# An attention and gated-MLP kernel: own places in SBUF for the first chunk's q, k and v, its k issued from ScalarE's queue, and a retuned order of work

## The chip, the cores and the metric

The kernel runs on one core of a Trainium2 chip. The metric is the device time of one execution in microseconds; three runs of the kernel before gave 740.18, 741.96 and 742.35 us, median 741.96 us. A profiled execution gives a trace of every instruction on the core's engines: PE (TensorE, matrix products and transposes; PEld are its weight loads), DVE (VectorE), ACT (ScalarE), POOL (GpSimd) and SP (SyncE, which here only issues transfers).

## What is computed

Attention over 4 batches, 8 heads, 768 positions and a head size of 64, masked to a causal window of 128 positions plus 4 sink positions; then its output, as 3072 tokens of 512 numbers, goes through a dense layer of 512 x 2048, the gate h * cos(h), and a second dense layer of 2048 x 512. Cut to what matters:

```python
scores = scale * np.matmul(q, k.transpose(0, 1, 3, 2))
keep = is_sink | in_window
scores = np.where(keep, scores, -1000000000.0)
a = np.exp(scores - np.max(scores, axis=-1, keepdims=True))
a = a / (np.sum(a, axis=-1, keepdims=True) + 1e-09)
x = np.matmul(a, v).transpose(0, 2, 1, 3).reshape(B * S, H * D)
h = x @ w_in
g = h * np.cos(h)
return g @ w_out
```

q, k and v arrive as float32, the two weights as 64-bit floats, decoded to float32 on the chip.

## The kernel before

The tokens are worked in 12 chunks of 256. For each chunk the attention of 8 heads is done, in pairs of heads, and then the dense part, in 8 slots of 256 hidden columns each. A slot is 24 products of the first layer (`h_mm`, L419), the gate on ACT and DVE (L428 to L464), and 24 products of the second layer (`out_mm`, L479). Each float32 operand is split into a high and a low part, and three products stand for one. Chunk 0 is an exception: its second layer uses unsplit float32 (L474), because the second weights are split only later.

The first three chunks are the "early" ones: they are the first 256 tokens of batches 0, 1 and 2, 24 heads in all. For a pair of early heads, q and k are loaded in rows (`load_natural`, L817, two transfers each), turned by PE (`pe_turn`, L825), copied out of PSUM (`q_out`, `k_out`, both through the helper at L407 for ACT and L409 for DVE), multiplied to scores (`scores_pe`, L850), masked on DVE (L919), exponentiated on ACT (L928), normalised (`norm`, L947; ACT L951, DVE or POOL L953), turned again (L1025), copied (L407, L409) and multiplied with v (L1077). Other chunks work per head, with split operands (L906, L1021, L1101).

All pairs share one tile for q (`xq`), one for k (`xk`) and one for v (`v32`): a load for the next pair waits until PE has turned the present one. All of these loads are issued by SP.

At the same time the weights are loaded in 32 pieces of 512 KB (`weight_piece`, L524), decoded by three instructions on DVE (L540, L546, L552) and split by one on ACT (L579) and one on DVE or POOL (L582).

The order in which each engine does this is not written by hand. A planner (`Plan.order`, L70) takes steps with a list of engines that may do them, an estimated duration, what they depend on, and a due time; it runs through time and gives each engine, as it comes free, the step with the smallest due time of those that are ready. The due times and the penalties for a choice of engine are worked out from the table `C` (L28). 160 small products of no use (`fill`, L1375, tile `idle`) have the latest due times of all, so they stand wherever the planner sees PE with nothing else to do. On the chip each engine runs its list in order, and waits by semaphores.

The first product of the dense part (slot 0) writes the PSUM bank `b4`, which the turned probabilities of every odd head of chunk 0 use before; so it comes after the last head of chunk 0 is turned and copied out.

Of the kernel before, what the change touches and what calls it, by code (L numbers as in the profile page):

```python
# [9 lines left out]
F32 = mybir.dt.float32  # L10
# [17 lines left out]
C = {  # L28
# [3 lines left out]
    "NWF": 0.232, "PB": 5, "PEN": 27.684, "PL": 3, "POOLF": 4.428, "POOLPEN": -1.361, "QE": 5.937, "R": 2, "RAW": 2,  # L32
# [3 lines left out]
}  # L36
# [133 lines left out]
def attn_moe_kernel(ctx, tc, q, k, v, n_sink, window, w_in, w_out, out):  # L170
# [401 lines left out]

    def split_piece(plan, prio, w, ready, before):


        add = plan.add

        def round_hi(e):
            nc.scalar.copy(out=w.high(), in_=w.w32)  # L579

        def rest_lo(e):
            e.tensor_tensor(out=w.low(), in0=w.w32, in1=f32(w.hi), op=ALU.subtract)  # L582

        s4 = add((("ACT", act(WP)),), round_hi, [ready], prio)
        return [s4, add(sub(WP), rest_lo, [s4, *before], prio, port=True)]
# [87 lines left out]
    def banded_path():  # L673
# [119 lines left out]
        def load_v_pair(o, o1):  # L793
            def fn(e):
                dst = v32_t.rearrange("p a n d -> p (a n d)")[:, : o.nkb * 2 * D]
                o.v2 = o1.v2 = dst.rearrange("p (n c) -> p n c", c=2 * D)
                for h in range(2):
                    nc.sync.dma_start(
                        out=dst.rearrange("p (n h d) -> p n h d", n=o.nkb, d=D)[:, :, h, :],
                        in_=v[o.b, o.h + h, o.kb0 * P : (o.kb0 + o.nkb) * P, :].rearrange("(n s) d -> s n d", s=P),  # L800
                    )
            return fn
# [9 lines left out]
        def load_natural(tile, src, n):  # L812
# [5 lines left out]
            return fn  # L818

        def pe_turn(o, part, tile, n):  # L820
            def fn(e):
                if part == 0:
                    o.qk = ps.tile([P, 2, NT], F32, name=f"qk_{o.tag}", tag="b3")
                for m in range(n):
                    nc.tensor.transpose(  # L825
                        out=o.qk[:, part, m * P : (m + 1) * P],
                        in_=tile.rearrange("p a b -> p (a b)")[:, m * 2 * D : (m + 1) * 2 * D], identity=ident,
                    )
            return fn
# [310 lines left out]
        first = None  # L1140
        vs_last = None
        waiting = []

        def before_softmax(g, o):
# [19 lines left out]
            if o.early:  # L1164
                if o.odd == 0:
                    bx, bb, o.btq = buf("xq", 1), buf("b3", 1), buf("tq", 1)
                    src = lambda c: q[o.b, o.h + c, o.i0 * P : o.i0 * P + NT, :]
                    i = add(dma(2), load_natural(xq_t, src, CB), [bx], t - 8 * T + DQ + 0.4 if g else -2000.0, lat=2.3)
                    i = qt = add([("PE", 0.23)], pe_turn(o, 0, xq_t, CB), [i, bb], t - 6 * T + DQ + 0.3)
                    bx.users.append(i)  # L1170
                    q0 = add([("ACT", act(NT, False)), ("DVE", dve(NT))], q_out(o), [i, o.btq], t - 6 * T + DQ + 0.6)
                    bb.users.append(q0)
                    bx, o.bkz = buf("xk", 1), buf("kz", 1)
                    src = lambda c: k[o.b, o.h + c, o.kb0 * P : (o.kb0 + o.nkb) * P, :]
                    i = add(
                        dma(2), load_natural(xk_t, src, o.nkb), [bx], t - 7 * T + DQ + 1.2 if g else -1999.0, lat=2.4
                    )
                    i = add(
                        [("PE", 0.115 * o.nkb)], pe_turn(o, 1, xk_t, o.nkb), [i, qt],
                        t - 6 * T + DQ + 1.0,  # L1180
                    )
                    bx.users.append(i)
                    kk = []
# [90 lines left out]
        def after_softmax(g, o):  # L1274
            x, t = xs[o.a], head_time(g)
            T, DV, DA = (C["TQ"], C["VE"], C["AE"]) if o.early else (C["T"], C["DV"], C["DA"])
            if o.early and o.odd == 0:
                o.bxs = [buf("v32", C["XV"]) for _ in range(C["XV"])]
                o.vl = add(dma(2), load_v_pair(o, heads[g + 1]), o.bxs, t - 2 * T + DV + 3.2, lat=2.4)
# [4 lines left out]
            if o.early:  # L1284
# [12 lines left out]
                )  # L1297
                x.y0 = y0
                for bx in bxs:
                    bx.users.append(y0)  # L1300
# [116 lines left out]
        for t, a, s in slots:  # L1417
# [4 lines left out]
            for m in range(0 if a else FG):  # L1422
                f = s * FG + m
                prio = slot_time(1, s) + C["SO"] + C["SO2"] * m
                pair = split_piece(plan, prio, w_outs[f], w_out_ready[s][f], before["out"])
                before["out"] = pair + xs[0].om[f]
# [181 lines left out]
```

## Time and profile before

| what | us |
|---|---|
| median of three runs | 741.96 |
| the profiled execution | 743.21 |
| span of its trace | 741.5 |
| PE busy in the span | 724.8 |
| DVE busy | 627.9 |
| ACT busy | 557.7 |
| POOL busy | 106.6 |

The span goes from the first to the last instruction of the program. Busy is the time in which an engine works on at least one instruction; on PE the ends of products are modelled and neighbours overlap, so the distance from one start to the next tells more than the duration of one. The granted clock of TensorE is full in every slice until the last few microseconds.

### The profile page before, as it was taken

What the parts mean: (1) busy time and instruction counts of PE and PEld (TensorE: products, weight loads), DVE (VectorE), ACT (ScalarE), POOL (GpSimd) and SP (SyncE); (2) the same over time, 40 slices, a digit from 0 to 9 for tenths busy, and PEclk for the clock granted to TensorE, in tenths of its full rate; (3) what the DMA queues carried; (4) which work ended last, traced back from release to release, by engine and by line L of the source; (5) the groups of instructions that cost most, each with busy time, mean ns of one, the idle gap of its engine ahead of it and who ended that gap; (6) DMA issues with size and microseconds to landing.
All of it is one profiled execution on the core that took longest, in us unless ns stands there. A gap on an engine that the chain in (4) does not pass through costs nothing.

```text
span 741.5 us, 15107 instructions
## 1 busy us (share of the span) xinstructions
PE 724.8 (98%) x4827; PEld 645.5 (87%) x4827; DVE 627.9 (85%) x1778; ACT 557.7 (75%) x1387; POOL 106.6 (14%) x191
## 2 busy tenths in 40 slices
PE   9989999999999999999999999999999999999996
PEld 8777776799999998998998889999998999999995
DVE  6899999877899999999999999897988888965432
ACT  4889969556979778799797898887888698884322
POOL 1000000001121221212212122122001122212000
PEclk9999999999999999999999999999999999999999
DMA  5755566132355455465465442232342232110000
GB/s 148 199 169 185 165 179 171 55 49 41 97 144 130 97 149 135 99 171 120 113 157 159 95 106 52 56 67 42 53 88 48 45 80 51 33 40 8 30 1 32
DMA packets 215896, 71.48 MB, mean 96 GB/s; under 512 B 204288, under 2 KB 204800, under 8 KB 215808
## 3 DMA queue, kind: packets, MB, share of 16 engines
q1 hardware_dynamic: 215376, 70.36, 39.1%
q8 instruction: 40, 0.66, 0.4%
q14 instruction: 48, 0.39, 0.2%
q10 hardware_dynamic: 432, 0.07, 0.0%
HBM read 64.10 MB, written 6.29 MB: 95 GB/s over the span
## 4 chain that ended last, share of the span: by engine, by line
PE 80%; DVE 9%; ACT 7%; DMA 1%; issue 1%; POOL 0%; SPq 0%; DVEq 0%; POOLq 0%; ACTq 0%
PE h L419 33%; PE acc L479 31%; PE av L1101 5%; PE s L906 4%; PE tp L1021 2%; PE idle L1379 1%; ACT p L928 1%; ACT p L951 1%; DVE p L919 1%; DVE w_out L546 1%; PE acc L474 1%; DVE w_out L552 1%; PE av L1077 1%; DVE lo_in L582 1%; ACT r L441 1%
## 5 line engine op out<-in xcount | busy, mean ns | idle before, releaser
L419 PE MATMUL h<-xhi,hi_in 128*128 128x256 f32 x768 | 226.0, 294 | 2.6 <-ACT firsts L407 1.4
L419 PE MATMUL h<-xlo,hi_in 128*128 128x256 f32 x768 | 217.0, 282 | 0.4 <-DVE xlo L365 0.4
L419 PE MATMUL h<-xhi,lo_in 128*128 128x256 f32 x768 | 216.7, 282 | 0.0
L419 PEld LDWEIGHTS h<-xhi,hi_in 128*128 128x128 f32 x768 | 146.0, 190 | 7.8 <-DVE glo L464 1.8
L419 PEld LDWEIGHTS h<-xhi,lo_in 128*128 128x128 f32 x768 | 146.3, 191 | 3.2 <-issue 1.1
L419 PEld LDWEIGHTS h<-xlo,hi_in 128*128 128x128 f32 x768 | 146.1, 190 | 0.6 <-DVE xlo L365 0.6
L479 PE MATMUL acc<-hi_out,ghi 128*128 128x512 f32 x350 | 142.2, 406 | 0.2 <-ACT raw L407 0.2
L479 PE MATMUL acc<-lo_out,ghi 128*128 128x512 f32 x350 | 137.4, 393 | 0.0
L479 PE MATMUL acc<-hi_out,glo 128*128 128x512 f32 x350 | 137.4, 392 | 0.0
L1060 POOL TENSOR_SCALAR_AFFINE_SELECT pz<-pz 128x512 fp32r<-128x512 f32 x128 | 83.4, 652 | 285.1 <-DVE pz L1047 221.0
L919 DVE CUSTOM_DVE_ANT_0 p<-s,mk 128x264 f32<-128x264 f32 (+1 forms) x192 | 75.7, 401 | 24.9 <-PE s L906 19.8
L428 ACT ACTIVATE yt<-h 128x512 int32<-128x512 f32 x96 | 57.2, 596 | 49.9 <-PE h L419 49.4
L928 ACT ACTIVATE p<-p,st 128x264 f32<-128x264 f32 (+1 forms) x192 | 93.6, 491 | 0.6
L434 DVE SCALAR_TENSOR_TENSOR r<-h,yt 128x512 f32<-128x512 f32 x96 | 65.5, 683 | 25.8 <-ACT yt L428 25.5
L441 ACT ACTIVATE r<-r,neg 128x512 f32<-128x512 f32 x96 | 69.3, 724 | 13.9 <-DVE r L434 13.1
L479 PEld LDWEIGHTS acc<-hi_out,glo 128*128 128x128 f32 x350 | 65.8, 188 | 14.8
L479 PEld LDWEIGHTS acc<-hi_out,ghi 128*128 128x128 f32 x350 | 65.9, 188 | 8.7 <-ACT raw L407 0.7
L479 PEld LDWEIGHTS acc<-lo_out,ghi 128*128 128x128 f32 x350 | 66.1, 189 | 7.6
L464 DVE TENSOR_TENSOR glo<-h,ghi 128x512 fp32r<-128x512 f32 x88 | 60.1, 683 | 11.6 <-ACT ghi L458 10.9
L446 DVE TENSOR_TENSOR h<-h,r 128x512 f32<-128x512 f32 x88 | 60.4, 687 | 8.2 <-ACT r L441 8.0
L458 ACT CAST ghi<-h 128x512 fp32r<-128x512 f32 x88 | 51.3, 583 | 16.1 <-PE acc L479 12.9
L906 PE MATMUL s<-r,l 128*128 128x264 f32 (+2 forms) x288 | 59.6, 288 | 0.8 <-DVE st L919 0.7
(140 smaller groups left out, 1288.5 us busy)
## 6 DMA issues: line engine op xcount, KB each, us to landing
raw<-in_moe_w_in_dram SPq DMA_DIRECT2D x32, 512.0 KB
raw<-in_moe_w_out_dram SPq DMA_DIRECT2D x32, 512.0 KB
xk<-in_k_dram SPq DMA_DIRECT2D x256, 48.0 KB
v<-in_v_dram SPq DMA_DIRECT2D x64, 96.0 KB
out_dram<-raw SPq DMA_DIRECT2D x22, 256.0 KB
xq<-in_q_dram SPq DMA_DIRECT2D x144, 32.0 KB
v<-in_v_dram SPq DMA_DIRECT2D x32, 64.0 KB
xq<-in_q_dram SPq DMA_DIRECT2D x24, 64.0 KB
```

The source lines that it names most:

```text
L419: nc.tensor.matmul(out=o.h[:, t, :], lhsT=w[:, fs], rhs=xx[:, c, :], start=(c == 0 and n == 0), stop=(c == NC - 1 and n == 2),)
L428: nc.scalar.activation(out=yt, in_=o.h, func=AF.Copy, scale=INV2PI, bias=0.25)
L434: nc.vector.scalar_tensor_tensor(out=o.r, in0=o.h, scalar=INV2PI, in1=yt, op0=ALU.mult, op1=ALU.subtract)
L441: nc.scalar.activation(out=o.r, in_=o.r, func=AF.Sin, scale=TWOPI_DOWN, bias=quarter)
L446: nc.vector.tensor_tensor(out=o.h, in0=o.h, in1=o.r, op=ALU.mult)
L458: nc.scalar.copy(out=o.ghi, in_=o.h)
L464: e.tensor_tensor(out=o.glo, in0=o.h, in1=f32(o.ghi), op=ALU.subtract)
L479: nc.tensor.matmul(out=x.acc[j], lhsT=gg[:, t, j * P : (j + 1) * P], rhs=w, start=(f == 0 and n == 0), stop=(f == NFT - 1 and n == 2), ski ...
L906: nc.tensor.matmul(out=o.s_ps[j][:, :w], lhsT=o.l[:, j * P : (j + 1) * P], rhs=r.rearrange("p n s -> p (n s)")[:, c0 : c0 + w], start=(n = ...
L919: nc.vector.tensor_tensor_reduce(out=o.p[:, j, :w], in0=o.s_ps[j][:, :w], in1=masks[min(o.i0 + j, 2)][:, :w], op0=ALU.add, op1=ALU.min, sc ...
L928: nc.scalar.activation(out=o.p[:, j, :w], in_=o.p[:, j, :w], func=AF.Exp, bias=o.lead.st[:, 0, o.nth, j : j + 1], scale=-1.0, accum_out=o. ...
L1060: nc.gpsimd.affine_select(out=env.pz4[:, :, :, n], in_=f32(env.pz4)[:, :, :, 0], pattern=[[0, 2], [0, CB], [sign, P]], compare_op=ALU.is_g ...
```

## The change

The first chunk's q and k of a pair get a tile of their own, and its v another (`early`). These tiles lie where the high parts of the last eight second weights come later (tags `a_out_8` to `a_out_15`), so the split of those weights (`split_piece`) now also waits for the last reader of the place (`rooms`). The loads of chunk 0 no longer wait for an earlier pair. Its q is issued by SP at due times of the table (`XP`), its k by ACT's queue ahead of its first work, its v by SP. The later early chunks keep the shared tiles. At the same time most numbers of the table `C` that set due times and the choice of engine are other ones; a few lines of it are shown.

```diff
-    "NWF": 0.232, "PB": 5, "PEN": 27.684, "PL": 3, "POOLF": 4.428, "POOLPEN": -1.361, "QE": 5.937, "R": 2, "RAW": 2,
-    "S0": -10.291, "S1": 61.51, "SAME": -0.554, "SE": -1.813, "SEM": 0.31, "SO": 6.105, "SO2": 1.36, "SPE": 0.183,
...
+    "NWF": 0.799, "PB": 5, "PEN": 24.474, "PL": 3, "POOLF": 12.358, "POOLPEN": -0.716, "QE": 8.165, "R": 2, "RAW": 2,
+    "S0": -10.709, "S1": 63.509, "SAME": -0.646, "SE": -1.186, "SEM": 0.209, "SO": 5.845, "SO2": 1.36, "SPE": 0.171,
...
+    "WO": 19.92, "WS": 1.465, "WS2": -0.01, "WT": 2, "XE": 2.209, "XP": [-2229.806, -1906.19, -1330.4, -570.267],
...
-        s4 = add((("ACT", act(WP)),), round_hi, [ready], prio)
+        s4 = add((("ACT", act(WP)),), round_hi, [ready, *room], prio)
...
-                dst = v32_t.rearrange("p a n d -> p (a n d)")[:, : o.nkb * 2 * D]
+                dst = (v32_t.rearrange("p a n d -> p (a n d)") if o.a else early(o, 1))[:, : o.nkb * 2 * D]
...
+        def early(o, n):
+            if not hasattr(o, "room"):
+                o.room = {}
+            if n not in o.room:
+                m = NFT - 2 * NP + 2 * o.pair + n
+                o.room[n] = wp.tile([P, WP], F32, name=f"room_{m}", tag=f"a_out_{m}")
+            return o.room[n]
+
+        def load_first(o, part, src, n):
+            def fn(e):
+                dst = early(o, 0)[:, part * NT : part * NT + n * 2 * D]
+                dst = dst.rearrange("p (n h d) -> p n h d", n=n, d=D)
+                for h in range(2):
+                    e.dma_start(out=dst[:, :, h, :], in_=src(h).rearrange("(n s) d -> s n d", s=P))
+            return fn
...
-                    i = add(dma(2), load_natural(xq_t, src, CB), [bx], t - 8 * T + DQ + 0.4 if g else -2000.0, lat=2.3)
+                    if o.a:
+                        i = add(dma(2), load_natural(xq_t, src, CB), [bx], t - 8 * T + DQ + 0.4, lat=2.3)
+                    else:
+                        i = add(dma(2), load_first(o, 0, src, CB), [], C["XP"][o.pair], lat=2.3)
...
+                    if o.a:
+                        i = add(dma(2), load_natural(xk_t, src, o.nkb), [bx], t - 7 * T + DQ + 1.2, lat=2.4)
+                    else:
+                        i = add([("ACT", 0.8)], load_first(o, 1, src, o.nkb), [], -2990.0 + o.pair, lat=2.4)
...
-                pair = split_piece(plan, prio, w_outs[f], w_out_ready[s][f], before["out"])
+                pair = split_piece(plan, prio, w_outs[f], w_out_ready[s][f], before["out"], rooms[f])
```

What this does to the lists of two engines stands in three places below. The first is the head of SP's list, the issues of transfers. `xq`, `xk` and `v` are the shared tiles, `room` the new ones, `raw` a weight piece as it comes from memory, `xb` the sink rows of v. Before:

```order
L817 DMA xq<-in_q_dram 128x2x64 x2
L817 DMA xk<-in_k_dram 128x2x64 x2
L532 DMA raw_70<-in_moe_w_in_dram 128x1024
L532 DMA raw_71<-in_moe_w_in_dram 128x1024
L798 DMA v_74<-in_v_dram 128x2x64 x2
L747 DMA xb<-in_v_dram 32x1x64 x4
L817 DMA xq<-in_q_dram 128x2x64 x2
```

And now:

```order
L835 DMA room_127<-in_q_dram 128x2x64 x2
L835 DMA room_130<-in_q_dram 128x2x64 x2
L835 DMA room_135<-in_q_dram 128x2x64 x2
L533 DMA raw_70<-in_moe_w_in_dram 128x1024
L533 DMA raw_71<-in_moe_w_in_dram 128x1024
L835 DMA room_156<-in_q_dram 128x2x64 x2
L818 DMA xq<-in_q_dram 128x2x64 x2
L818 DMA xk<-in_k_dram 128x2x64 x2
```

Three pairs' q now stand ahead of the first weight piece, and the four pairs' k have left this list for ACT's, where they stand behind the load of the exp table and the one small activation that follows it (L255 before), and ahead of all other work.

The second place is the head of PE's list, from the products of no use (`idle`) to the second pair's scores. `qk_0_0` is the PSUM tile of the first pair's turned q and k, `qk_0_2` that of the second; `s_0_0_0` and `s_0_0_1` are the two halves of the first pair's scores. Before:

```order
L1379 MATMUL idle<-gt 128x256 x8
L825 MATMUL qk_0_0_144<-ident,xq 128x128 x2
L1379 MATMUL idle<-gt 128x256 x7
L825 MATMUL qk_0_0_144<-ident,xk 128x128 x2
L1379 MATMUL idle<-gt 128x256 x13
L850 MATMUL s_0_0_0_188<-firsts,tq_0_0_154 128x2x128
L850 MATMUL s_0_0_1_192<-firsts,tq_0_0_154 128x512
L1379 MATMUL idle<-gt 128x256 x13
L825 MATMUL qk_0_2_218<-ident,xq 128x128 x2
L1379 MATMUL idle<-gt 128x256 x7
L825 MATMUL qk_0_2_218<-ident,xk 128x128 x2
```

And now:

```order
L1420 MATMUL idle<-gt 128x256 x8
L844 MATMUL qk_0_0_153<-ident,room_127 128x128 x2
L1420 MATMUL idle<-gt 128x256 x14
L844 MATMUL qk_0_0_153<-ident,room_127 128x128 x2
L1420 MATMUL idle<-gt 128x256 x11
L877 MATMUL s_0_0_0_212<-firsts,tq_0_0_161 128x2x128
L844 MATMUL qk_0_2_214<-ident,room_130 128x128 x4
L877 MATMUL s_0_0_1_222<-firsts,tq_0_0_161 128x512
L1420 MATMUL idle<-gt 128x256 x13
L877 MATMUL s_0_2_0_258<-firsts,tq_0_2_236 128x2x128
```

The second pair is turned right behind the first half of the first pair's scores, where 20 products of no use and the other half stood between; between the first pair's q and its k there are now 14 of them and not 7.

The third place is PE's list just ahead of slot 0's first product (`h`). `av` are the products with v of chunk 0's pairs, the one at L354 subtracts a pair's high part. Before, these are rows 71 to 79 of the list:

```order
L825 MATMUL qk_0_6_655<-ident,xq 128x128 x2
L1379 MATMUL idle<-gt 128x256
L850 MATMUL s_0_4_0_662<-firsts,tq_0_4_638 128x2x128
L354 MATMUL av_0_4_603<-xhi_397,gt 128x512
L825 MATMUL qk_0_6_655<-ident,xk 128x128 x2
L1379 MATMUL idle<-gt 128x256 x9
L1077 MATMUL av_0_6_698<-firsts,v_74 128x256
L1077 MATMUL av_0_6_698<-firsts,v_74 128x128
L419 MATMUL h_710<-xhi_397,hi_in_263 128x256
```

Now they are rows 56 to 64:

```order
L1052 MATMUL tp_0_7_566<-ident,p_0_7_410 128x128 x3
L1104 MATMUL av_0_4_540<-firsts,room_227 128x256
L1104 MATMUL av_0_4_540<-firsts,room_227 128x128
L877 MATMUL s_0_2_1_581<-firsts,tq_0_2_537 128x512
L1104 MATMUL av_0_6_589<-firsts,room_217 128x256
L1104 MATMUL av_0_6_589<-firsts,room_217 128x128
L355 MATMUL av_0_4_540<-xhi_427,gt 128x512
L1420 MATMUL idle<-gt 128x256 x8
L420 MATMUL h_613<-xhi_427,hi_in_282 128x256
```

Slot 0's first product has moved from row 79 to row 64: 108 of the 160 products of no use now stand ahead of it, where all 160 did. Of chunk 1's second pair of early heads (`s_0_2`) only the scores are done there, not those of the third (`s_0_4`). The other 52 stand behind it, all of them ahead of slot 4.

## Rows read from the trace of the kernel before

**Rows 1.** The page: busy us, share of the span and instructions of each engine.

```profile
span 741.5 us, 15107 instructions
PE 724.8 (98%) x4827; PEld 645.5 (87%) x4827; DVE 627.9 (85%) x1778; ACT 557.7 (75%) x1387; POOL 106.6 (14%) x191
```

**Rows 2.** Windows: stretch in us, its length, busy us and instructions per engine.

```profile
core 0: us, PE busy (x) PEld busy (x) DVE busy (x) ACT busy (x) POOL busy (x), PEclk, DMA share, GB/s
0.00:50.00 50.00, 45.21 (x286) 38.94 (x287) 40.53 (x141) 34.66 (x108) 3.24 (x12) 1.00 0.62 173
50.00:130.00 80.00, 77.14 (x425) 57.09 (x425) 76.09 (x183) 66.67 (x164) 0.00 (x0) 1.00 0.60 173
130.00:500.00 370.00, 367.16 (x2521) 333.87 (x2520) 339.32 (x995) 295.21 (x732) 70.44 (x120) 1.00 0.45 105
```

**Rows 3.** Timeline: slot 0's first product, and that of the tenth slot.

```profile
49.36 0.39 PE L419 MATMUL h<-xhi,hi_in 128*128 128x256 f32 x1 [1.37 <-ACT firsts L407]
...
127.10 0.39 PE L419 MATMUL h<-xhi,hi_in 128*128 128x256 f32 x1 [0.22 <-DVE g L452]
```

**Rows 4.** Chain that ended last, in order of time: start, us, what.

```profile
1.42 2.09 PE warm L240 x8
...
3.56 2.08 PE idle L1379 x8
...
10.82 1.55 PE idle L1379 x13
...
15.44 1.29 PE s L850 x4
...
17.40 4.56 DMA xq<-in_q_dram
...
134.57 1.72 PE acc L474 x4
...
138.04 2.88 PE h L419 x24
```

**Rows 5.** Waits of PE until 130 us: total us, times, longest.

```profile
PE warm L240 <- POOL ident L230: 1.4, 1, 1.4
PE h L419 <- ACT firsts L407: 1.4, 1, 1.4
PE s L850 <- DVE st L919: 1.1, 3, 0.7
PE qk L825 <- DMA xq<-in_q_dram: 1.0, 1, 1.0
PE tp L1025 <- ACT p L951: 0.7, 2, 0.4
...
PE h L419 <- DVE g L452: 0.2, 1, 0.2
```

**Rows 6.** Timeline: issues of transfers by SP, and ACT's start.

```profile
0.81 0.97 SPq L817 DMA_DIRECT2D xq<-in_q_dram  x2
1.81 0.98 SPq L817 DMA_DIRECT2D xk<-in_k_dram  x2
...
3.04 0.20 ACT L255 ACTIVATE flag<-neg 1x1 f32<-1x1 f32 x1
...
8.62 1.70 SPq L817 DMA_DIRECT2D xq<-in_q_dram  x2
...
16.98 0.89 SPq L817 DMA_DIRECT2D xq<-in_q_dram  x2
```

**Rows 7.** Groups on DVE until 130 us: busy us, mean ns | idle before.

```profile
L409 DVE COPY firsts<-tp 128x384 f32<-128x384 f32 x6 | 3.3, 554 | 0.3 <-ACT p L928 0.2
L409 DVE COPY firsts<-qk 64x256 f32<-64x256 f32 x6 | 2.5, 424 | 0.2
```

**Rows 8.** Groups over the span: normalisations on POOL and ACT.

```profile
L953 POOL TENSOR_SCALAR p<-p,st 128x136 f32<-128x136 f32 x29 | 13.0, 457 | 82.6 <-DVE st L943 52.5 <-DVE p L936 16.0 <-ACT yt L428 7.4
L951 ACT ACTIVATE p<-p,st 128x136 f32<-128x136 f32 x64 | 22.2, 400 | 1.7 <-DVE st L943 1.7
```

**Rows 9.** Waits of PE from 130 us to the end, first and last of five.

```profile
PE h L419 <- DVE glo L464: 1.0, 2, 0.7
...
PE acc L479 <- ACT raw L407: 0.2, 1, 0.2
```

More of the change, by code (lines that the diff above doesn't have):

```diff
@@ L571, in weight_piece, with split_piece @@
         return s3
-    def split_piece(plan, prio, w, ready, before):
+    def split_piece(plan, prio, w, ready, before, room=()):
         add = plan.add
@@ L818, in load_natural @@
             return fn
+        def early(o, n):
[12 more added lines that the diff above has]
+            return fn
         def pe_turn(o, part, tile, n):
             def fn(e):
+                if tile is None:
+                    if part == 0:
+                        o.qk = ps.tile([P, 2, NT], F32, name=f"qk_{o.tag}", tag="b3")
+                    for m in range(n):
+                        nc.tensor.transpose(
+                            out=o.qk[:, part, m * P : (m + 1) * P],
+                            in_=early(o, 0)[:, part * NT + m * 2 * D : part * NT + (m + 1) * 2 * D], identity=ident,
+                        )
+                    return
                 if part == 0:
@@ L1141, in banded_path @@
         vs_last = None
+        rooms = [[] for _ in range(NFT)]
         waiting = []
@@ L1165, in before_softmax @@
                 if o.odd == 0:
-                    bx, bb, o.btq = buf("xq", 1), buf("b3", 1), buf("tq", 1)
+                    bx = buf("xq", 1) if o.a else None
+                    bb, o.btq = buf("b3", 1), buf("tq", 1)
                     src = lambda c: q[o.b, o.h + c, o.i0 * P : o.i0 * P + NT, :]
-                    i = add(dma(2), load_natural(xq_t, src, CB), [bx], t - 8 * T + DQ + 0.4 if g else -2000.0, lat=2.3)
-                    i = qt = add([("PE", 0.23)], pe_turn(o, 0, xq_t, CB), [i, bb], t - 6 * T + DQ + 0.3)
@@ L1170, in before_softmax @@
-                    bx.users.append(i)
+                    if o.a:
+                        i = add(dma(2), load_natural(xq_t, src, CB), [bx], t - 8 * T + DQ + 0.4, lat=2.3)
+                    else:
+                        i = add(dma(2), load_first(o, 0, src, CB), [], C["XP"][o.pair], lat=2.3)
+                    i = qt = add([("PE", 0.23)], pe_turn(o, 0, xq_t if o.a else None, CB), [i, bb], t - 6 * T + DQ + 0.3)
+                    if o.a:
+                        bx.users.append(i)
+                    else:
+                        rooms[NFT - 2 * NP + 2 * o.pair].append(i)
@@ L1171, in before_softmax @@
                     q0 = add([("ACT", act(NT, False)), ("DVE", dve(NT))], q_out(o), [i, o.btq], t - 6 * T + DQ + 0.6)
                     bb.users.append(q0)
-                    bx, o.bkz = buf("xk", 1), buf("kz", 1)
+                    bx, o.bkz = buf("xk", 1) if o.a else None, buf("kz", 1)
                     src = lambda c: k[o.b, o.h + c, o.kb0 * P : (o.kb0 + o.nkb) * P, :]
+                    if o.a:
+                        i = add(dma(2), load_natural(xk_t, src, o.nkb), [bx], t - 7 * T + DQ + 1.2, lat=2.4)
+                    else:
+                        i = add([("ACT", 0.8)], load_first(o, 1, src, o.nkb), [], -2990.0 + o.pair, lat=2.4)
@@ L1175, in before_softmax @@
                     i = add(
[L1176 to L1179, printed above, removed]
+                        [("PE", 0.115 * o.nkb)], pe_turn(o, 1, xk_t if o.a else None, o.nkb), [i, qt],
                         t - 6 * T + DQ + 1.0,
                     )
-                    bx.users.append(i)
+                    if o.a:
+                        bx.users.append(i)
+                    else:
+                        rooms[NFT - 2 * NP + 2 * o.pair].append(i)
@@ L1277, in after_softmax @@
             if o.early and o.odd == 0:
-                o.bxs = [buf("v32", C["XV"]) for _ in range(C["XV"])]
+                o.bxs = [buf("v32", C["XV"]) for _ in range(C["XV"])] if o.a else []
                 o.vl = add(dma(2), load_v_pair(o, heads[g + 1]), o.bxs, t - 2 * T + DV + 3.2, lat=2.4)
@@ L1298, in after_softmax @@
                 x.y0 = y0
+                if o.a == 0:
+                    rooms[NFT - 2 * NP + 2 * o.pair + 1].append(y0)
                 for bx in bxs:
```

10 rows, old and new, of the table C are left out of this document.

## The prediction

> **What bounds the kernel now.** I read first the page's busy shares: PE works in 98% of the span, DVE in 85%, ACT in 75% [rows 1]. So the end is set by how early PE gets its work and by how little it waits. The windows then tell where it does not run full: PE is idle for 4.8 us of the first 50 us, 2.9 us of the next 80 and 2.8 us of the 370 after that [rows 2]. But the first stretch is worse than it looks, since most of PE's 45.2 us there are the 160 products of no use. Thirteen of them take 1.55 us in the chain, 0.12 us each [rows 4], so all cost 19.1 us. DVE is the second limit: in the 80 us from 50 on it is busy for 76.1 us [rows 2], and the chain that ended last runs there through both engines.
>
> The third view is the timeline: slot 0's first product starts at 49.36 us, after a wait of 1.37 us on ACT, and the tenth slot's first product at 127.10 us [rows 3].
>
> The tenth slot is the place where the two orders can be compared. I counted what stands ahead of it in PE's list, and the count is the same before and after: 160 products of no use, 216 of the first layer, 25 of the unsplit second layer, 24 score products, 48 transposes of q and k, 66 of probabilities, 42 products with v and 10 subtractions. At the chain's distances (24 products of a slot's first layer in 2.88 us, four halves of L474 in 1.72 us, a pair's scores in 1.29 us, [rows 4]; the other kinds, by their distances in the timeline, at 0.11 to 0.43 us apiece) this is 111 us of work. PE got there at 127.1 us. So 16 us are all that a better order of the first part can win, and the 160 products of no use are no part of it: they stand in the list in both cases, and moving 52 of them behind slot 0 only defers them. Of the 16 us, 1.4 pass before the first instruction, and the warming products and the first idle ones are slow (8 in 2.1 us each, [rows 4]), which costs another 3. Nothing in the change touches these. Some 11 us are left, of which the trace names 6.0 us as waits of PE: nine rows, 7.4 us together, less the 1.4 us at the very start [rows 5].
>
> **The change part by part.** *The loads of q.* Before, each pair's load waits until the shared tile is free: the second pair's q is issued at 8.62 us and the fourth's at 16.98 us, from which the chain waits 4.56 us for its landing [rows 4, 6]. On PE this shows as 1.0 us of waiting for xq [rows 5]; the rest lies under products of no use. With tiles of their own the three first q are issued back to back at some 0.97 us each, by 3.7 us, and the fourth after two weight pieces, near 5.6 us, over 10 us before its use. The wait of 1.0 us goes: -1.0. What is late next is DVE.
>
> *Slot 0.* Its first product waits 1.37 us for the copy of chunk 0's last odd head [rows 3]. In ACT's new list this copy stands ahead of the eight exponentials of chunk 1 that stood ahead of it. PE's list has 7.1 us less ahead of slot 0 (52 products of no use, 6.2 us, and 0.9 us of transposes and scores), so I put slot 0 at 41 to 43 us. The 1.4 us of waiting goes, but the lead does not stay: by slot 4 the new list has 5 us more ahead than the old one, and by slot 9 the same. Term: -1.4.
>
> *The loads of k on ACT's queue.* The first pair's k was issued at 1.81 us; now it comes behind the small activation at 3.04 to 3.24 us [rows 6], 1.4 us later. Seven more products of no use stand in front of its turning, at the slow rate of the start (2.08 us for 8, [rows 4]), which would cover it; but then these set the time. I put the first scores 0.9 us later than before; the bounds are 0 and 1.4. ACT issues eight transfers at about 0.45 us until 6.9 us, and its first copy before the change was at about the same time, so nothing queued behind them is late. Term: +0.9. On SP, the first weight pieces are issued 0.9 us later and the later pieces stand behind ten loads for chunks 0 and 1; DVE needs the first piece only after the first masks, so I cost this at nothing; if that cover is gone, it is up to 1 us on DVE.
>
> [...] No transfer of this size on ACT's queue is in the trace before.
>
> *The work on DVE.* In the new lists 2 of the six copies of turned probabilities, 3 of those of q and k, and 2 of the splits of x leave DVE for ACT. At 554 and 424 ns [rows 7], and 418 for the last kind as an estimate from the like copy, this is 3.2 us; two more normalisations come to DVE in this part, at 0.3 us. DVE's list ahead of the tenth slot's first gate step is thus 2.6 us shorter, on an engine that is 95% busy there [rows 2]. Of the 3.6 us of PE's named waits that are left (6.0 - 1.0 - 1.4), most are on DVE or on ACT behind it. The bounds of this term are 0 (PE's own list decides) and -3.6 (all these waits go). I take -2.0, nearer to DVE's 2.6 than to 0.
>
> *The new due times after the tenth slot.* All 33 normalisations on POOL go: 35 more of the 136-column ones are on ACT, 0.40 us each against 0.46 [rows 8]. ACT is busy for 295 of 370 us in the middle [rows 2]; 14 us more make it 84%. PE's list has the same work; its named waits there are 2.7 us in five rows [rows 9]. I take 0, between -2.7 and +3.5 (a quarter of ACT's 14 us, an estimate, reaching PE). The rooms cost nothing: the splits of the last second weights come after chunk 0's last product with v.
>
> **Sum.** -1.0 - 1.4 + 0.9 - 2.0 = -3.5 us against the profiled execution's 743.21 us. This is 1.25 us above the median of the runs, so I apply the difference to the median: 741.96 - 3.5 = 738.5 us. The bounds of the terms: -1.0 - 1.4 - 3.6 - 2.7 = -8.7, or 733.3 us; and +1.4 + 3.5 with the waits of slot 0 and q replaced by others, or 746.9 us, though not all of these together.
>
> **Rivals.** *The lead is kept.* Slot 0 comes some 7 us earlier and the work of slots 4 and 5, which DVE had been late for, fills in without waits. Then PE's unnamed gaps go too, and the gain is 7.5 us: 734.5 us. For it: counted from the lists with the durations of the groups, DVE has 5 us less ahead of slot 0's first gate step. Against it: PE's list to the tenth slot is the same length, and half of the 11 us is no named wait.
>
> *The gain is given back by the tenth slot.* DVE's whole work of the first 130 us is but 2.6 us shorter, and it idles only 9.5 us of the first 50 [rows 2], mostly at the start, which the change lengthens by 0.9. The new list has 4.6 us more of DVE's work ahead of slot 5's gate than the old one, so PE would wait there for what it did not wait for before: 741.5 to 742.5 us, 742 taken. This is also the case in which own places for loads do nothing that shows, as the loads were hidden under products of no use.
>
> *ACT becomes late in the middle.* Place: the normalisations of each group of four heads, which ACT now does one behind the other ahead of the transposes on PE. Price: with 37 normalisations more, 0.4 us each, a quarter to a half on PE's path gives 3.7 to 7.4 us, less the 3.5 of the start: +2 to +4, so 745 us. It decides once ACT, which makes the copies that PE waits for, is over some 95% busy in a stretch of the middle; it is at 80% [rows 2], which speaks against it; that DVE had taken normalisations beside POOL speaks for it.
>
> **How the numbers follow.** A measurement here tells a change from none at about 0.3%, or 2.2 us. My forecast, 736 to 741 with 738.5 the middle, gets 0.45, the kept lead 0.14, the gain given back 0.26, ACT late in the middle 0.15. Faster by over 0.3% (below 739.7) holds 0.40 of the first, all of the second and 0.02 of the third: 0.56. Slower by over 0.3% (above 744.2) holds most of the last and 0.02 of the third: 0.14. The rest, 0.30, is no change that can be measured. The range of 8 in 10 goes from 733.5, near the sum of all good bounds, to 744.5, which leaves out the worse half of the last case.
>
> **What would show it.** Right: slot 0's first product near 42 us without a wait on ACT; no wait of PE for a q of chunk 0; the tenth slot's first product at 123 to 124.5 us; named waits of PE to 130 us at 3 us or less; the middle from 130 to 500 us with PE idle for about 3 us. Wrong: first scores later than 10.8 us, or DVE's mask of the first pair beyond 11.5 us (k late); the tenth slot at 127 us or later (given back); at 121 us (kept); or PE idle for over 6 us between 130 and 700 us with waits on ACT L951 (ACT late).

## The result, and the profile after

The changed kernel takes 745.96 us (median of 7 runs, 744.48 to 747.25); the kernel before, beside it, 742.46 us. The ratio is 1.0051, with a 95% interval of 1.0036 to 1.0067: slower by 3.5 us, where 3.5 us of gain from 741.96 had been forecast. 745.96 lies 1.5 us above the upper end of the range.

The page of the changed kernel, busy us, share of the span and instructions, against [rows 1]:

```profile
span 743.8 us, 15011 instructions
PE 726.0 (98%) x4827; PEld 644.8 (87%) x4827; DVE 627.1 (84%) x1781; ACT 570.8 (77%) x1435; POOL 88.8 (12%) x140
```

The work moved as the lists said: over the whole span ACT has 13 us more, POOL 18 less, DVE 0.8 less. Its windows, first the three of [rows 2], then two of 10 us:

```profile
0.00:50.00 50.00, 43.72 (x266) 37.17 (x266) 35.95 (x135) 34.79 (x108) 2.86 (x11) 0.97 0.57 156
50.00:130.00 80.00, 76.40 (x427) 57.24 (x428) 75.81 (x182) 69.02 (x168) 0.00 (x0) 1.00 0.62 183
130.00:500.00 370.00, 368.33 (x2528) 334.06 (x2528) 338.63 (x988) 299.62 (x755) 59.65 (x89) 1.00 0.45 105
...
20.00:30.00 10.00, 6.73 (x41) 5.38 (x40) 6.60 (x28) 7.24 (x26) 0.00 (x0) 0.95 0.60 185
30.00:40.00 10.00, 9.69 (x58) 8.43 (x57) 8.70 (x28) 8.94 (x25) 0.00 (x0) 0.88 0.44 134
```

The middle is no worse: PE idles 1.7 of 370 us, against 2.8. The first 50 us are where the loss is. DVE is busy there for 35.95 us, against 40.53, and between 20 and 30 us PE, DVE and ACT all stand still for about a third of the time. The timeline of SP's issues, the counterpart of [rows 6], tells why:

```profile
0.80 3.07 SPq L835 DMA_DIRECT2D room<-in_q_dram  x6
4.75 1.57 SPq L533 DMA_DIRECT2D raw<-in_moe_w_in_dram  x2
8.93 0.89 SPq L835 DMA_DIRECT2D room<-in_q_dram  x2
...
12.75 0.98 SPq L799 DMA_DIRECT2D v<-in_v_dram  x2
13.78 4.05 SPq L799 DMA_DIRECT2D room<-in_v_dram  x8
17.95 2.86 SPq L748 DMA_DIRECT2D xb<-in_v_dram  x4
20.92 0.86 SPq L533 DMA_DIRECT2D raw<-in_moe_w_in_dram  x2
```

The third weight piece is issued at 20.92 us, in the last of these rows. Before, its row was this:

```profile
14.61 0.98 SPq L532 DMA_DIRECT2D raw<-in_moe_w_in_dram  x2
```

Eight loads of chunk 0's v (4.05 us), which now need not wait for a place, and the four of the sinks' v (2.86 us) stand in front of it. DVE's timeline has the consequence, and behind it the copy that PE needs:

```profile
25.16 0.43 DVE L541 TENSOR_SCALAR w_in<-raw 128x512 int32<-128x512 int32 x1 [2.62 <-DMA raw<-in_moe_w_in_dram]
...
27.71 0.43 DVE L410 COPY firsts<-qk 64x256 f32<-64x256 f32 x1
```

PE's timeline, where the last two rows answer to [rows 3]:

```profile
9.06 0.67 PE L877 MATMUL s<-firsts,tq 128*128 128x256 f32 x2 [0.16 <-ACT firsts L408]
...
10.92 0.41 PE L844 MATMUL qk<-ident,room 128*128 128x128 f32 x2 [0.97 <-DMA room<-in_k_dram]
...
28.29 0.67 PE L877 MATMUL s<-firsts,tq 128*128 128x256 f32 x2 [2.67 <-DVE firsts L410]
...
43.82 0.39 PE L420 MATMUL h<-xhi,hi_in 128*128 128x256 f32 x1
...
129.61 0.39 PE L420 MATMUL h<-xhi,hi_in 128*128 128x256 f32 x1
```

Slot 0 starts 5.5 us earlier and waits for nothing, but the tenth slot comes 2.5 us later (127.10 before), with the same work ahead of it. The 2.67 us are now the largest of PE's waits to 130 us; the first five rows, as in [rows 5]:

```profile
PE s L877 <- DVE firsts L410: 2.7, 1, 2.7
PE h L420 <- DVE g L453: 1.4, 2, 1.0
PE warm L241 <- POOL ident L231: 1.4, 1, 1.4
PE s L877 <- ACT firsts L408: 1.4, 4, 0.6
PE qk L844 <- DMA room<-in_k_dram: 1.0, 1, 1.0
```

Behind the stall the granted clock is lower, too. In windows of 1 us it is the column ahead of the last two, with 1.00 for full speed:

```profile
28.00:29.00 1.00, 0.71 (x4) 0.64 (x5) 0.94 (x5) 1.00 (x5) 0.00 (x0) 1.00 0.80 193
29.00:30.00 1.00, 1.00 (x7) 1.00 (x6) 0.97 (x2) 1.00 (x6) 0.00 (x0) 0.53 0.79 315
30.00:31.00 1.00, 1.00 (x5) 0.82 (x4) 1.00 (x2) 0.76 (x3) 0.00 (x0) 0.50 0.49 123
31.00:32.00 1.00, 1.00 (x7) 1.00 (x6) 0.38 (x1) 0.47 (x3) 0.00 (x0) 0.50 0.54 124
32.00:33.00 1.00, 1.00 (x8) 1.00 (x8) 0.96 (x5) 0.98 (x4) 0.00 (x0) 0.76 0.79 175
```

For some 3.4 us PE was granted 0.50 of full speed: 0.47 + 0.50 + 0.50 + 0.24 = 1.7 us of full speed lost, as an estimate from these rows.

### The profile page after: what moved, and what is told of

It is laid out like the page before. It is cut to its first block, busy times and chain, and to the rows that moved or that the text cites. A ratio compares the mean times of both kernels' runs of the same rounds, so it can differ in the third digit from the quotient of the medians.

```text
span 743.8 us, 15011 instructions
## 1 busy us (share of the span) xinstructions
PE 726.0 (98%) x4827; PEld 644.8 (87%) x4827; DVE 627.1 (84%) x1781; ACT 570.8 (77%) x1435; POOL 88.8 (12%) x140
## 4 chain that ended last, share of the span: by engine, by line
PE 74%; DVE 10%; ACT 8%; DMA 3%; issue 2%; SPq 2%; DVEq 0%; ACTq 0%
PE h L420 31%; PE acc L480 28%; PE av L1128 5%; PE s L933 4%; PE tp L1048 2%; ACT p L955 1%; DMA raw<-in_moe_w_in_dram 1%; PE av L1104 1%; ACT p L978 1%; DVE r L435 1%; PE acc L475 1%; PE tp L1052 1%; DVE p L946 1%; ACT firsts L408 1%; DMA room<-in_k_dram 1%
## 5 line engine op out<-in xcount | busy, mean ns | idle before, releaser
L1087 POOL TENSOR_SCALAR_AFFINE_SELECT pz<-pz 128x512 fp32r<-128x512 f32 x128 | 85.6, 669 | 454.6 <-DVE pz L1074 419.8
```

The source lines that it names most:

```text
L1087: nc.gpsimd.affine_select(out=env.pz4[:, :, :, n], in_=f32(env.pz4)[:, :, :, 0], pattern=[[0, 2], [0, CB], [sign, P]], compare_op=ALU.is_g ...
```

## The experiments

Each kernel ran beside the kernel before. "Tenth" is the start of the tenth slot's first product in its profiled execution (before: 127.10 us).

| run | median us (runs) | ratio | 95% | tenth |
|---|---|---|---|---|
| changed | 745.96 (7) | 1.0051 | 1.0036-1.0067 | 129.61 |
| changed again (e12) | 747.17 (6) | 1.0065 | 1.0047-1.0084 | 129.54 |
| e1 | 742.55 (11) | 1.0007 | 0.9997-1.0017 | 128.05 |
| e2 | 749.70 (5) | 1.0089 | 1.0075-1.0104 | 135.42 |
| e3 | 750.46 (4) | 1.0106 | 1.0091-1.0121 | 135.40 |
| e4 | 746.78 (6) | 1.0058 | 1.0037-1.0078 | 131.59 |
| e5 | 742.93 (11) | 1.0007 | 0.9996-1.0018 | 126.44 |
| e6 | 743.31 (11) | 1.0018 | 1.0009-1.0028 | 126.22 |
| e7 | 749.09 (4) | 1.0090 | 1.0074-1.0105 | 133.28 |
| e8 | 758.80 (5) | 1.0218 | 1.0204-1.0232 | 136.06 |
| e9 | 741.77 (12) | 0.9991 | 0.9980-1.0001 | 126.97 |
| e11 | 743.92 (10) | 1.0015 | 1.0005-1.0024 | 127.25 |
| e13 | 740.30 (12) | 0.9971 | 0.9959-0.9984 | 124.09 |
| e14 | 741.67 (11) | 0.9993 | 0.9983-1.0002 | 126.29 |
| e15 | 741.24 (11) | 0.9983 | 0.9974-0.9992 | 124.03 |
| e16 | 742.77 (11) | 1.0004 | 0.9995-1.0013 | 125.89 |

### SP's list: e1, e11, e12

The planner's list is taken as it is, and only a few of SP's steps are put elsewhere in it. e1:

```diff
-        emit(plan.order(BEGIN), setup)
+        rows = plan.order(BEGIN)
+        at = [n for n, r in enumerate(rows) if getattr(r[2], "raw", False)][3] + 1
+        late = [r for r in rows[:at] if getattr(r[2], "late", False)]   # v of pairs 2 and 3, sinks' v
+        emit([r for r in rows[:at] if r not in late] + late + rows[at:], setup)
```

> The changed kernel with one difference: on SP's queue the third and fourth weight piece are issued ahead of two of chunk 0's four v pairs and of the four loads of the sinks' v; every other engine's order is word for word that of the changed kernel. Theory (SP starves the VectorE of weight pieces): the third piece is issued at about 16 us instead of 20.92, VectorE's 2.62 us wait at 25.16 falls below 0.7, TensorE's 2.67 us wait at 28.29 below 0.7, its clock between 20 and 40 us is 1.00 again, and the time falls by 2.7 (that wait) to 4.4 us (with 0.05 and 0.12 of two stretches of 10 us given back by the clock): 741.6 to 743.3. Rival (the new table's order, or the work moved to ScalarE, is what costs): the waits move, the time stays within 1 us of 745.96.

It takes 742.55 us, 0.44% less than the changed kernel by the two ratios: 3.3 us. That is inside what the theory expected. DVE's waits for pieces, 2.62 and 1.36 us in the changed kernel, fell to this row of DVE's waits until 50 us:

```profile
DVE w_in L543 <- DMA raw<-in_moe_w_in_dram: 0.6, 1, 0.6
```

The clock between 20 and 40 us is full (1.00), but the profiled execution lost some at another place: PE waited 1.60 us for the second pair's k, until 11.54 us, and in the four windows of 1 us from 11 to 15 us its granted clock was 0.81, 0.50, 0.50 and 0.50. e11 moves four issues only, the sinks' v, behind the sixth piece, and e12 repeats the changed kernel beside it:

> The changed kernel with one edit: the four loads of the sinks' v behind the sixth weight piece; chunk 0's eight v loads stay ahead of the third. Theory: the third piece is issued 3.0 us earlier, at about 18 instead of 20.92, VectorE's 2.62 us wait at 25 us falls to under 0.8 and the time by 2.5 to 4: 742 to 743.5. Rival (the eight v loads, 4.05 us, are what is in the way): 744.3 to 746.

> The changed kernel once more, on this chip beside the two above: 745.5 to 746.5 by every theory, so that they can be compared with it.

In e11 SP's rows for the third piece and for the sinks' v are these:

```profile
17.93 0.86 SPq L533 DMA_DIRECT2D raw<-in_moe_w_in_dram  x2
...
29.23 2.86 SPq L750 DMA_DIRECT2D xb<-in_v_dram  x4
```

The third piece comes 3.0 us earlier, DVE's waits for pieces fall to 1.4 us, and the time is 743.92 us, beside 747.17 of e12: 3.2 us less by the medians. It is 0.4 us above what the theory gave and short of what the rival gave. So four loads of 8 KB, first used at 41 us in e11, cost some 3 us by standing where they stood. Four of the v loads ahead of them, moved in e1 as well, add little: the intervals of e1 and e11 overlap. In e12 PE did not wait for the second pair's k at all, and yet the tenth slot came at 129.54, since the wait behind the third piece grew:

```profile
28.02 0.67 PE L877 MATMUL s<-firsts,tq 128*128 128x256 f32 x2 [3.38 <-DVE firsts L410]
```

So the wait for k does not make the loss.

### Either half alone: e2, e3

```diff
-    "NWF": 0.799, "PB": 5, "PEN": 24.474, "PL": 3, "POOLF": 12.358, "POOLPEN": -0.716, "QE": 8.165, "R": 2, "RAW": 2,
+    "NWF": 0.232, "PB": 5, "PEN": 27.684, "PL": 3, "POOLF": 4.428, "POOLPEN": -1.361, "QE": 5.937, "R": 2, "RAW": 2,
...
+    "WO": 17.592, "WS": 1.821, "WS2": -0.01, "WT": 2, "XE": 2.85, "XP": [-2229.806, -1906.19, -1330.4, -570.267], "XV": 2,
```

This is e2, against the changed kernel. e3 is the kernel before with the changed kernel's numbers in their place.

> The new places for chunk 0's q, k and v and k by ScalarE's queue, with the numbers of the old table (the four due times of the q loads added, since the code needs them). SP's list has the same head as in the changed kernel: eight v loads and four of the sinks' v ahead of the third weight piece. Theory (SP starves VectorE): the third piece is issued at 20 to 21.5 us, VectorE waits over 2 us for it, and the kernel is slower than before by 1.5 to 5 us: 744 to 747.5. Rival (the new table costs it): without the new table the kernel is level with before or faster, 739 to 742.5.

> The kernel before with the new table of numbers alone: chunk 0's q, k and v in the old single buffers, all loads on SP. On SP's list only the eight loads of two q and k pairs stand between the second and the third weight piece. Theory (SP starves VectorE because of the new places): no such wait, level with before within 2 us: 740.5 to 744.5, VectorE waits under 1 us for weight pieces until 50 us. Rival (the new table costs it): slower than before by 2.5 to 4 us, 745 to 746.5.

e2 has the wait expected (one of 5.0 us on DVE for the third piece) and is slower than expected, at 749.70. e3 went against my theory: 750.46 us, with 0.4 us of DVE waiting for pieces until 50 us. PE's waits from 50 to 100 us in e3 say where:

```profile
PE av L1078 <- ACT firsts L408: 2.0, 2, 1.3
PE h L420 <- ACT firsts L408: 0.8, 1, 0.8
PE tp L1026 <- DVE firsts L410: 0.7, 1, 0.7
```

So the new numbers do not fit the old places: there the products with v and slot 0 wait for copies. And the granted clock is lower in two stretches of 4 us, 0.57 on average in each. The column ahead of the last two again:

```profile
51.00:55.00 4.00, 3.85 (x12) 2.75 (x12) 2.61 (x7) 0.83 (x4) 0.00 (x0) 0.57 0.33 95
78.00:82.00 4.00, 3.65 (x9) 1.99 (x9) 2.75 (x9) 3.10 (x7) 0.00 (x0) 0.57 0.34 89
```

That is 3.4 us of full speed lost, as an estimate, of the 8.3 us by which e3's tenth slot is late. e2 loses as much in two such stretches (mean clock 0.57 from 27 to 31 us, 0.66 from 105 to 110). Each half alone costs 7 to 8 us, both together 3.5. "The table" and "the places" cannot be priced one by one.

### k's queue: e4, e5, e6

```diff
-                    e.dma_start(out=dst[:, :, h, :], in_=src(h).rearrange("(n s) d -> s n d", s=P))
+                    nc.sync.dma_start(out=dst[:, :, h, :], in_=src(h).rearrange("(n s) d -> s n d", s=P))
```

This edit of `load_first` is in e4 and e5: k is issued by SP. In e6 it stays on ACT's queue.

> The changed kernel with chunk 0's k loads on SP's queue instead of ScalarE's; the orders are otherwise those of the changed kernel. Theory (SP's queue is the bound at the start): eight more issues of 0.47 us stand ahead of the weight pieces, four of them ahead of the first two, so the first piece is 1.9 us later and the third 3.8 us later than in the changed kernel, VectorE waits 6 us or more for pieces until 30 us, and the time is 747.5 to 750. Rival (ScalarE's 4.33 us of issues cost it): ScalarE's first copies start earlier, the time falls by 1 to 2 us to 744 to 745.

> Both edits on SP's list: chunk 0's k by SP (the second pair's k ahead of the first weight piece, as in e4, where TensorE was busy 10.00 of 10 us from 10 to 20 us), and the third and fourth weight piece ahead of two v pairs and the sinks' v (as in e1). The other engines' orders are those of the changed kernel, ScalarE's without the eight issues. Theory now: two things at the start cost the changed kernel its gain, late weight pieces (VectorE) and the second pair's k, which lands behind 1 MB of weights (TensorE's 0.97 us wait at 10.92, 1.60 in e1). Without both: no wait of TensorE for k, VectorE's waits for pieces under 2 us (the third is issued at about 18), 739.5 to 742. Rival (k by ScalarE's queue is worth its place, SP's 3.8 us of issues are the larger evil): VectorE waits over 3 us for pieces, 744 or more.

> e1 with the second weight piece issued behind the last q pair instead of right behind the first piece; k stays on ScalarE's queue. Theory (the second pair's k lands late because two pieces of 512 KB are in flight with it): TensorE's wait for it (1.60 us in e1, 0.97 in the changed kernel) falls by at least 0.7, and the time to 740.5 to 742; the second piece, used at 14.7 to 16.9 us, lands in time. Rival (the second pair's k is late because ScalarE issues it late, 4 to 5 us): the wait stays within 0.3 us, the time at 742 to 743.5.

e4: DVE waits 6.3 us for pieces, as expected, but the time is 0.7 us under the range and that of the changed kernel within the intervals; the third piece came only 1.1 us later (22.05 us), since in the changed kernel SP had stood idle from 6.3 to 8.9 us, a time that k's issues now fill. PE waited 5.44 us behind that piece, and the tenth slot came 2.0 us later than in the changed kernel. e5 has e1's edit as well, missed its 739.5 to 742, and did not get below e1: the wait for k is gone, and in its place PE waits 1.67 and 0.42 us at 26 us for q and k of chunk 1, which stand behind the sinks' v. In e6 the wait only moved to the first pair: ACT's seven issues took 6.32 us instead of 4.33, and the first scores came at 11.05. Neither queue for k is worth a measurable amount.

### The cost given to the kernel before: e7

```diff
+        at = [n for n, r in enumerate(rows) if getattr(r[2], "raw", False)][2]
+        again = [r for r in rows if getattr(r[2], "sinks", False)][0]
...
+        emit(rows[:at] + [again] * 2 + rows[at:], setup)
```

> The kernel before with the four loads of the sinks' v issued twice more (the same data again, eight issues, 5.7 us of SP) ahead of its third weight piece; no other engine's order changes. Theory (late pieces are enough to cost it): the third piece is issued at about 20 us instead of 14.61 and the two q and k pairs behind it as much later, VectorE waits 2 to 5 us more, and the kernel is slower than before by 2 to 5 us: 744.5 to 747.5. Rival (the kernel before has slack there, the loss of the changed kernel is the table's): within 1 us of before.

749.09 us: 0.90% or 6.7 us slower, more than expected. SP's and PE's timeline:

```profile
14.62 5.58 SPq L749 DMA_DIRECT2D xb<-in_v_dram  x8
20.25 0.91 SPq L532 DMA_DIRECT2D raw<-in_moe_w_in_dram  x2
...
26.16 0.66 PE L828 MATMUL qk<-ident,xq 128*128 128x128 f32 x2 [5.05 <-DMA xq<-in_q_dram]
```

DVE waited 5.1 us for the piece; PE's own wait is for the q loads that stand behind it. The clock was lower too, 0.62 on average from 23 to 32 us, which is 3.4 us of full speed. So SP's place in this stretch is dear in both kernels, but e7 doesn't separate the pieces from the q.

### ScalarE in the middle: e8

```diff
-    "LAG": 4.632, "LB": 88.715, "LEAD": 1.034, "LP": -0.072, "NE": 0.194, "NEH": 24, "NM": 1.796, "NW": 5.237,
-    "NWF": 0.799, "PB": 5, "PEN": 24.474, "PL": 3, "POOLF": 12.358, "POOLPEN": -0.716, "QE": 8.165, "R": 2, "RAW": 2,
+    "LAG": 4.632, "LB": 88.715, "LEAD": 1.034, "LP": -0.072, "NE": 0.194, "NEH": 24, "NM": 1.796, "NW": 1.863,
+    "NWF": 0.232, "PB": 5, "PEN": 24.474, "PL": 3, "POOLF": 4.428, "POOLPEN": -1.361, "QE": 8.165, "R": 2, "RAW": 2,
```

> The changed kernel with the four numbers that keep work off GpSimd (NW, NWF, POOLF, POOLPEN) at their old values: 40 normalisations are GpSimd's again and ScalarE has 33 fewer; SP's list has the same head, with twelve loads ahead of the third weight piece. Theory (SP starves VectorE at the start): VectorE still waits over 2 us for the third piece at 22 to 26 us, 744.5 to 748. Rival (ScalarE is late in the middle): the time falls to 741 to 743.

758.80 us, neither theory's number. SP's head is the same, DVE waits 4.6 us for pieces and the tenth slot is 9.0 us later than in the kernel before. Another 12.6 us are lost between the 37th and the 49th slot, where the clock is at 0.50 from 390 to 396 us, and the largest of PE's waits from 130 us is this:

```profile
PE tp L1048 <- DVE p L980: 4.7, 1, 4.7
```

With GpSimd's normalisations back, the middle of the new order is much worse, so nothing here speaks for the rival. But the four numbers change the order of the first part too (the tenth slot is 6.5 us later than in the changed kernel), and e8 does not price ScalarE's share alone.

### What takes the rest: e9, e13, e14

e9 is e5 with the sinks' v behind the sixth piece.

> e5 (k by SP, third and fourth weight piece ahead of two v pairs) with the four loads of the sinks' v (3.49 us of SP in e5, first used at 43 us) put behind the sixth weight piece; no other engine's order changes. Theory (what is left of the loss at the start is SP's list again: in e5 TensorE waits 1.67 and 0.42 us at 26 us for q and k of chunk 1, issued at 23.47 behind the sinks' v): these two waits fall below 0.4 in sum, and the time is 2.1 us under e5's 742.93: 740 to 741.5, under both kernels. Rival (these waits are given back later, by VectorE's g between 104 and 120 us): 742 to 743.5.

741.77 us, between the two expectations: under the changed kernel by 0.6%, level with the one before. Both waits at 26 us are gone and slot 0 starts at 39.48 us, and still the tenth slot is at 126.97. The starts of slots' first products show where the lead goes:

| kernel | first | seventh | tenth | last |
|---|---|---|---|---|
| before | 49.36 | 104.61 | 127.10 | 720.34 |
| changed | 43.82 | 106.37 | 129.61 | 723.28 |
| e9 | 39.48 | 102.64 | 126.97 | 720.62 |
| e13 | 40.12 | 102.48 | 124.09 | 718.20 |
| e15 | 39.00 | 101.07 | 124.03 | 719.39 |

Between the seventh and the tenth e9 gives back 1.8 of its 2.0 us. The windows of just this stretch, the kernel before, then e9:

```profile
104.61:127.10 22.49, 21.52 (x114) 15.18 (x112) 21.45 (x48) 17.79 (x44) 0.00 (x0) 1.00 0.70 195
```

```profile
102.64:126.97 24.33, 21.47 (x113) 14.94 (x111) 23.55 (x44) 18.16 (x41) 0.00 (x0) 1.00 0.67 184
```

PE has the same to do; DVE has 2.1 us more and is busy 97% of the time, against 95%. e9's groups on PE in it, with idle time and releaser:

```profile
L420 PE MATMUL h<-xhi,hi_in 128*128 128x256 f32 x25 | 7.9, 317 | 1.5 <-DVE g L453 1.5
L420 PE MATMUL h<-xhi,lo_in 128*128 128x256 f32 x24 | 7.0, 291 | 1.1 <-DVE lo_in L585 1.1
```

e13 and e14 leave out one of three bit operations on six pieces of the second weights there:

```diff
+        tops = [r for r in rows if getattr(r[2], "top", False)][24:30]
+        rows = [r for r in rows if r not in tops]
```

> e9 without one of the three bit operations (the one that puts the top bits in) on six pieces of the second weights, those at 106 to 123 us: 6 x 0.69 = 4.2 us less for VectorE, and those six pieces' values are wrong. All else stays. Theory (with SP's list mended the lead of 2.0 us that e9 has at the seventh product, 102.64 against 104.61 us, is given back because VectorE, busy 23.55 of the 24.33 us from there to the tenth, is the bound of that stretch): the tenth product comes 2 to 2.9 us earlier, at 124.1 to 125, TensorE's waits for g and lo_in in the stretch fall from 2.6 to under 0.7, and the time to 738.9 to 740. Rival (TensorE's own sequence, not VectorE, takes the lead back): under 0.7 us of change, 741.1 to 742.4.

> The kernel before with the same operation left out on the same six pieces (here at 107 to 122 us): 4.2 us less for VectorE. Theory: in the kernel before VectorE has 2.1 us less to do in this stretch and TensorE idles only 1.0 us in it, so 0.5 to 1.0 us is won: 741.4 to 741.9. Rival (VectorE binds this stretch alike in both): as much as in e13.

In e13 the same stretch is this:

```profile
102.48:124.09 21.61, 20.48 (x113) 15.00 (x111) 19.02 (x37) 16.73 (x38) 0.00 (x0) 1.00 0.68 191
```

It is 2.7 us shorter than in e9, PE no longer waits for g there, and the tenth slot comes at 124.09. At the last slot 2.4 us of the lead are left, and the time falls by 1.5 us to 740.30, just above the expected range. In e14 the stretch shortens by 0.5 us (22.00 after 22.49), and the time falls by 0.5 us, which its interval does not tell from nothing. So DVE is the bound of this stretch in the new order, and far less so in the old one.

### A version under both: e15, e16

```diff
+        lows = [r for r in rows if getattr(r[2], "out", False)][4:]      # low parts of second weights
+        rows = [r for r in rows if r not in lows]
+        opens = [r for r in rows if getattr(r[2], "opens", False)]       # first product of each slot
+        for n, r in enumerate(lows):
+            rows.insert(rows.index(opens[10 + n // 2]) + 1 + n % 2, r)
```

> e9, and on VectorE's list the low parts of the second weights, from the fifth piece on, put two behind the start of each product from the eleventh on (they are first used at 143 us for the first piece and from about 158 us for the fifth); nothing is left out, the other engines' orders are those of e9. Five of them (5 x 0.69 = 3.4 us) leave the stretch from the seventh to the tenth product. Theory (VectorE binds that stretch): the tenth product at 124 to 125 us instead of 126.97, and, VectorE having 31 us of slack from 130 to 500 us, most of it is kept: 739 to 740.6, under both kernels. Rival (what is moved is paid behind the tenth product, where VectorE is as full): 741.2 to 742.5.

> The kernel before with the same edit of VectorE's list (the low parts of the second weights from the fifth piece on behind the eleventh and later products). Theory (in the order before VectorE is not the bound there): 0.3 to 1.0 us under before, 741.3 to 742.2. Rival (the edit helps any order): as much as in e15.

e15 computes all and takes 741.24 us: 0.17% under the kernel before (interval 0.08 to 0.26%) and 0.7% under the changed one; its interval overlaps that of e9. Its tenth slot is at 124.03, as the theory said, but not for the theory's reason alone. Its seventh slot is already 1.6 us ahead of e9's, and the first of the moved operations stood behind that slot in e9 (111.74 us). The stretch itself is only 1.4 us shorter, and PE still waits 2.4 us for g and `lo_in` in it (2.6 in e9). The time is at the rival's edge: of 2.9 us against e9, 1.2 are left at the last slot, and PE's waits from 130 us now lead with

```profile
PE h L420 <- DVE glo L466: 1.9, 2, 1.1
```

(1.1 in e9). The same edit does nothing for the time of the kernel before (e16), though the stretch shortens there by 1.0 us (21.48). So what the moved operations are worth by themselves is not shown; that the new places and numbers, with SP's list and these operations moved, can be a little faster than the old ones, is.

## Why the prediction was wrong

**The step that failed** is the sentence on SP: "the later pieces stand behind ten loads for chunks 0 and 1 ... I cost this at nothing; if that cover is gone, it is up to 1 us on DVE". I priced the head of the list, up to the first pieces; these came 1.9 us later, not 0.9 (4.75 against 2.84 us), and nothing waited for them. But between the second and the third piece stand 20 issues, not ten (14 before), and the last twelve, chunk 0's v and the sinks' v, take from 13.78 to 20.81 us. From 6.32 to 8.93 and from 9.82 to 10.80 us SP issued nothing; no run tells what held it. DVE waited 2.62 us for the third piece, PE 2.67 us behind it, and the lower clock (0.50 for some 3.4 us) cost 1.7 us more, by the estimate from its windows: 4.4 us in the trace, against 0. Not all of it reaches the end: the tenth slot is 1.6 us earlier in e1, 2.4 in e11 and 2.6 in e9. e1 and e11 take back 3.2 to 3.3 us of the time by moving issues of SP alone, which is shown; that the lower clock is part of it rests on the windows, not on a run of its own.

**The second step** is the term of -2.0 for DVE. Its work was counted rightly. Here are the sums of windows from the start to the tenth slot's first product, before, changed, and e9:

```profile
sum 127.10, PE 119.61 PEld 93.51 DVE 113.82 ACT 99.47 POOL 3.24; mean PE 39.87 PEld 31.17 DVE 37.94 ACT 33.16 POOL 1.08
```

```profile
sum 129.61, PE 119.73 PEld 94.03 DVE 111.38 ACT 103.81 POOL 2.86; mean PE 39.91 PEld 31.34 DVE 37.13 ACT 34.60 POOL 0.95
```

```profile
sum 126.97, PE 119.12 PEld 93.02 DVE 111.64 ACT 103.98 POOL 2.87; mean PE 39.71 PEld 31.01 DVE 37.21 ACT 34.66 POOL 0.96
```

DVE has 2.4 us less to do (2.6 forecast). But it idles 18.2 us before the tenth slot in the changed kernel, against 13.3, and even with SP's list mended 15.3. By the seventh slot it has done 88.09 us of work in e9, against 92.36 before; from there to the tenth it has 23.55 to do, against 21.45. A shorter list on the bounding engine is only worth something if its work also comes in time; here more of it was left for the end. That DVE bounds this last stretch is shown by e13; why it falls behind ahead of the seventh slot was not tested.

**Point by point.** The -1.0 for chunk 0's q: no such wait is left, right. The -1.4 for slot 0: the wait on ACT is gone and 41 to 43 us was nearly met (43.82; 39.5 to 40.7 in e5 and e9). Both were swallowed further on, as the text on slot 0 itself warned. The +0.9 for k: the first scores came at 9.06 us (9.37 before), so it was near 0 for the first pair. Its premise held only in part. One of the eight issues went out ahead of the small activation, and the other seven took until 8.04 us, not 6.9:

```profile
1.80 0.46 ACTq L835 DMA_DIRECT2D room<-in_k_dram  x1
3.04 0.20 ACT L256 ACTIVATE flag<-neg 1x1 f32<-1x1 f32 x1
3.71 4.33 ACTq L835 DMA_DIRECT2D room<-in_k_dram  x7
```

The second pair's k made PE wait 0.97 us and not at all in two executions of the changed kernel, and 1.60 in e1. By e4 and e5, moving k between the two queues moved waits and no time that could be measured (1.0058 against 1.0051 for e4 and the changed kernel, 1.0007 for both e5 and e1).

The 0 for the middle: right, PE's waits there are 1.8 us in three rows, against 2.7 in five [rows 9], the first of them

```profile
PE h L420 <- DVE glo L465: 1.1, 1, 1.1
```

and that speaks against the rival of a late ACT, whose work from 130 to 500 us grew by 4.4 us only, to 81% of the time. That rival's sum also has a slip: 3.7 to 7.4 less 3.5 is +0.2 to +3.9, not +2 to +4. The comparison at the tenth slot held: what was lost there (2.5 us) is nearly all of the difference at the last slot (2.9).

Of the rivals, "given back by the tenth slot" was put at 742 us. With SP's list mended (e9, 741.77) that is what remains; the changed kernel itself is that rival plus a queue that I had not priced.

Open: why the old numbers on the new places (e2) lose 3.7 us more than the new ones, and what each of the waits and the two stretches at the lower clock adds to e3's 8 us; no run tells these apart.

## What to carry to other kernels

When a change frees loads from waiting for a place, they can come to stand ahead of loads that are needed sooner: read the whole stretch of the queue up to the next load that a busy engine waits for, and price it issue by issue. Four small loads put 11 us later (17.95 to 29.23 us) were worth most of the loss (743.92 us in e11 beside 747.17). And where two engines are both nearly full, count the second one's work stretch by stretch up to the same point: DVE's was shorter in sum in e9 (111.64 us after 113.82) but later, and it bound the last stretch, where it was busy for 23.55 of 24.33 us.

## What the runs showed of the hardware

In the changed kernel PE stood still for 2.67 us (25.6 to 28.3 us). In windows of 1 us its granted clock was 1.00 up to 29 us; 0.53, 0.50, 0.50 and 0.76 in the four from 29 to 33 us, with PE busy for the whole of each; and 1.00 in the next. In e1, where the wait of 1.60 us ended at 11.54 us, it was 0.81, 0.50, 0.50, 0.50 and 0.98 in the five from 11 to 16 us. In e5, with two waits of 1.67 and 0.42 us at 26 us, the windows of 10 us from 20 to 40 us show 1.00 and 1.00. In e4, with a wait of 5.44 us, they show 0.95 and 0.88, as in the changed kernel with 2.67 us. What sets the clock was not tested.

In the changed kernel the small sink loads of 8 KB took SP 0.72 us each to issue (2.86 us for four), the 64 KB loads of v 0.51 (4.05 for eight). The same head of a program gave waits for the second pair's k of 0.97 us and none in two executions of the changed kernel.
